# A delta-rule attention with a feed-forward behind it: the second inverse moved in front of the last weight conversion

## The chip, the cores and the metric

The kernel runs on one core of a Trainium2 chip. The metric is the device time of one execution, in microseconds (us). The kernel before takes 770.9 us (median of 3 runs, 770.83 to 771.04). The profile is of one more execution, which took 773.04 us; its span, from the first to the last instruction, is 771.3 us, and all positions in this document ("at 105 us") are counted from the start of a span.

The engines are called PE (TensorE, the matrix engine), DVE (VectorE), ACT (ScalarE), POOL (GpSimd) and SP (SyncE, which here only issues transfers).

## The reference, cut to what matters

For 4 batches and 8 heads, 768 positions of 48 values each, a state is updated by the delta rule:

```python
k_n = k / (np.linalg.norm(k, axis=-1, keepdims=True) + 1e-06)
for t in range(S):
    kt, vt, bt = (k_n[:, :, t], v[:, :, t], beta[:, :, t, None])
    y[:, :, t] = np.einsum('bhd,bhde->bhe', q[:, :, t], state)
    v_old = np.einsum('bhde,bhd->bhe', state, kt)
    state = state + bt[:, :, :, None] * np.einsum('bhd,bhe->bhde', kt, vt - v_old)
```

Its output, as 3072 rows of 384, goes through a feed-forward: `h = x @ w_in` (384 x 2048), `g = h * sigmoid(1.702 h)`, `out = g @ w_out` (2048 x 384). Everything is float32 in the kernel. `w_in` and `w_out` arrive as 64-bit floats, as two 32-bit words for each value, and the kernel builds the float32 values from the words itself.

## The kernel before, in words

**Units.** The 768 positions are cut into 6 chunks of 128. A chunk of one batch is a unit; units 0 to 3 are chunk 0, units 4 to 7 chunk 1, and so on. Inside a unit the delta rule is a triangular system. It is solved in four blocks of 32 positions: `solve` multiplies a block with the inverse of its 32x32 diagonal block (tile `XB`), ACT copies the result to `US`, `below` multiplies it with the Gram matrix `G` of the keys into `psR`, and `rest` (DVE) takes that off the values `V` of the blocks that follow. One such step of two interleaved units is called a hop (`hops`, `together`); eight hops solve a pair.

**Inverses.** `invert(c)` computes the 32x32 inverses of a chunk's units on DVE, with some 44 instructions that each follow from the one before. `invert(0)` is needed before the first hop; `invert(1)`, the second inverse, serves units 4 to 7. It reads the tile `NT`, which is filled by way of DRAM: for each unit, four transfers `Nd<-G` write the diagonal blocks of the Gram matrix, and one transfer `NT<-Nd` reads them back transposed. All of these are issued by SP.

**Keys.** `normalize_mixed` squares the keys on ACT (`ksq`), sums on DVE (`ssq`), takes the root on POOL (`rn`), and scales the keys on DVE. `prepare` then transposes them on PE (`psT`, copied to `kT`) and makes the Gram matrix (`psG`, copied to `G`), and issues the transfers to `NT`. The generator `keys` steps these for units 4 to 7 and for part of unit 8.

**Weights.** `conversions` turns the raw words into float32 on DVE, with one ACT operation per piece: 9 pieces of `w_in` (quarters 0, 1 and 3 of the 2048 columns are two pieces of 128x768 each, quarter 2 is three of 128x512) and then 14 pieces of `w_out` (twelve of 128x384, two of 128x768). `fill(n)` does n steps of that sequence; a piece has five steps. `fetch_in(3)`, the transfers of the last quarter of `w_in`, are issued by SP as soon as the second piece has been read.

**Feed-forward.** `hidden` makes `gT` for two batches; one step of it (`feed()`) is three products into `ph`, which the profile shows as 6 matmuls of 128x256, and it needs the attention output `xT`, whose last rows arrive through six transfers `xT<-last` that SP issues. `both_written(0, ...)` multiplies with `w_out` for two batches at once, in the order in which the pieces of `w_out` are converted.

**Order of the work.** The order on each engine is that of the program text for all that is pinned (`keep_in_program_order`), which is everything up to unit 8 or so; SP's transfers are pinned there as well. The part that the change touches is this sequence in the kernel's text:

1. loads, `invert(0)`, the first hops (units 0 and 1, line 1026), with `fill`, `keys` and `warm(11)` in every hop (`warm` is matmuls on nothing of use; each `warm(11)` is 11 of them),
2. `put_out` of units 0 and 1 (queries and state, PE tiles `psY`),
3. the second hops (units 2 and 3, line 1056), with `fill`, two steps of `keys`, and a `feed()` in each hop from the fourth on, `put_out` of units 2 and 3,
4. the scores of unit 4 (`first.scored`: tiles `QS`, `psQ`, `M`, and a subtraction from `V` on DVE),
5. `invert(1)` with 19 feeds beside it (line 1093),
6. the remaining feeds with the conversion of `w_out`, and then `woven`, which runs the steps of all further units with `both_written` and everything after it.

Scratch tiles of the tag `gT` are a ring of eight (`spare`), which `blocks` (the diagonal blocks of the first chunk), the raw words of quarter 2 and the `gT` tiles share. There are seven key tiles `KN`, so unit 7's keys need the tile of unit 0.

## Time and profile before

| what | value |
|---|---|
| median of 3 runs | 770.9 us |
| the profiled execution, its time | 773.04 us |
| the profiled execution, its span | 771.3 us |
| PE busy over the span | 751.0 us (97%) |
| DVE busy over the span | 440.6 us (57%) |
| ACT, POOL busy over the span | 241.3 us, 128.4 us |
| first hop begins, on PE | 42.1 us |
| second inverse, on DVE | 105.5 to 132.6 us |
| last instruction of the `w_out` conversion ends, on DVE | 172.4 us |
| `ps_warm` matmuls | 161 |

The page of the profile gives busy time for each engine, for the span and for forty slices of it (19.3 us each). The view by stretches gives busy time for stretches that the reader chooses. The view of waits says which engine stood still for whom. The chain of waits is followed back from the last instruction: at each step to what released it. A matmul that the program writes once in float32 is shown as two.

### The profile page before, as it was taken

Reading aid. Unit: us, or ns where it says so; the run is one execution under the profiler, and the core shown is the slowest. Engines: PE = TensorE matmul, PEld = TensorE weight load, DVE = VectorE, ACT = ScalarE, POOL = GpSimd, SP = SyncE. Lnnn points to the kernel's source line nnn. Section 1 sums busy time; section 2 is a strip of 40 time slices with the busy share of each in tenths; the row PEclk is TensorE's granted clock in tenths of the full one; section 3 lists DMA queues with packets and bytes.
Section 4 is the critical chain, followed back from the end, with each engine's and each line's share of the span. In section 5 each row is a group of like instructions: output and inputs, shape, how many; then the busy total and the mean of one; then the engine's idle time right before and its main releaser. Section 6 shows DMA issues by size and latency. Waiting matters only on the chain.

```text
span 771.3 us, 19547 instructions
## 1 busy us (share of the span) xinstructions
PE 751.0 (97%) x8545; PEld 563.6 (73%) x8545; DVE 440.6 (57%) x896; ACT 241.3 (31%) x535; POOL 128.4 (17%) x134
## 2 busy tenths in 40 slices
PE   7889999889999999999999999999999999999998
PEld 6678788556687688678678678678678677687684
DVE  5997879896875565665665665665665621000000
ACT  4555632343333233233223223233223123121110
POOL 6133310011221221220221221231210000000000
PEclk8588999999999999999999999999999999999999
DMA  9976550644342142142142042042030020000000
GB/s 158 176 119 144 123 97 21 165 101 97 77 108 57 35 95 57 35 97 56 27 103 56 23 107 58 23 98 66 22 77 12 23 45 1 17 11 1 26 1 20
DMA packets 130661, 50.78 MB, mean 66 GB/s; under 512 B 105408, under 2 KB 126016, under 8 KB 130576
## 3 DMA queue, kind: packets, MB, share of 16 engines
q1 hardware_dynamic: 128112, 41.08, 24.9%
q0 software_dynamic: 2464, 8.46, 4.6%
q8 instruction: 67, 1.10, 0.6%
q14 instruction: 18, 0.15, 0.1%
HBM read 32.08 MB, written 16.25 MB: 63 GB/s over the span
## 4 chain that ended last, share of the span: by engine, by line
PE 81%; DVE 10%; SPq 4%; ACT 2%; DMA 1%; issue 1%; POOL 0%; DVEq 0%; ACTq 0%
PE po L102 30%; PE ph L102 27%; PE psY L102 6%; PE psU L102 5%; SPq L102 4%; PE psQ L102 3%; PE psG L102 3%; PE psR L102 3%; DVE w_out L102 2%; DVE P L102 2%; PE psT L102 2%; PE ps_warm L102 2%; DVE tmp L102 2%; DVE YB L102 1%; DVE NT L102 1%
## 5 line engine op out<-in xcount | busy, mean ns | idle before, releaser
L102 PE MATMUL po<-w_out,gT 128*128 128x384 f32 x768 | 265.2, 493 | 3.6 <-ACT gT L102 1.9
L102 PE MATMUL ph<-xT,w_in 128*128 128x256 f32 x1152 | 260.9, 383 | 0.3
L102 PEld LDWEIGHTS ph<-xT,w_in 128*128 128x128 f32 x1152 | 214.9, 190 | 32.6 <-issue 1.7
L102 PEld LDWEIGHTS po<-w_out,gT 128*128 128x128 f32 x768 | 141.3, 190 | 94.2 <-issue 3.1
L102 DVE TENSOR_TENSOR V<-V,psR 128x384 f32<-128x384 f32 (+2 forms) x72 | 40.1, 558 | 193.6 <-PE psR L102 193.1
L102 ACT ACTIVATE gT<-ph 128x512 f32<-128x512 f32 x96 | 56.4, 595 | 138.9 <-PE ph L102 138.8
L102 DVE TENSOR_TENSOR P<-NT,YB 64x8 f32<-64x8 f32 (+26 forms) x178 | 86.0, 483 | 4.9
L102 ACT COPY US<-psU 32x384 f32<-32x384 f32 x92 | 43.1, 469 | 138.8 <-PE psR L102 81.6
L102 PEld LDWEIGHTS psU<-V,XB 32*32 32x32 f32 x1536 | 60.1, 106 | 34.6 <-issue 27.6
L102 DVE TENSOR_REDUCE YB<-P 64x4 f32<-64x8 f32 (+27 forms) x178 | 77.2, 434 | 6.1
L102 PE MATMUL psU<-V,XB 32*32 32x48 f32 x1536 | 71.5, 205 | 0.6 <-DVE V L102 0.4
L102 PE MATMUL psR<-US,G 32*32 32x48 f32 x2576 | 64.2, 205 | 1.5 <-ACT US L102 1.5
L624 POOL TENSOR_SCALAR_AFFINE_SELECT M<-M 128x1024 f32<-128x1024 f32 x20 | 25.5, 1276 | 225.6 <-DVE M L102 166.8
L102 PEld LDWEIGHTS psR<-US,G 32*32 32x32 f32 x2576 | 54.6, 105 | 2.8 <-ACT US L102 1.6
L102 PE MATMUL psQ<-QS,kT 48*128 48x176 f32 (+1 forms) x384 | 37.6, 341 | 3.7 <-ACT QS L102 3.7
L102 DVE TENSOR_TENSOR P<-NT 64x256 f32<-64x256 f32 (+7 forms) x44 | 36.3, 826 | 0.5
L102 DVE TENSOR_REDUCE NT<-P 64x64 f32<-64x1024 f32 (+7 forms) x44 | 35.3, 803 | 1.5
L102 PEld LDWEIGHTS psQ<-QS,kT 48*128 48x128 f32 x384 | 31.1, 209 | 6.8 <-ACT QS L102 5.5
L102 PE MATMUL psG<-kT 48*128 48x128 f32 x384 | 32.8, 309 | 2.7 <-ACT kT L102 1.4
L102 PEld LDWEIGHTS psG<-kT 48*128 48x128 f32 x384 | 27.6, 208 | 5.9 <-ACT G L102 2.2
L102 ACT COPY o<-po 128x384 f32<-128x384 f32 x24 | 11.5, 477 | 61.7 <-issue 39.2
L102 ACT COPY M<-psQ 128x256 f32<-128x256 f32 x68 | 22.8, 377 | 23.4 <-DVE V L102 17.3
(100 smaller groups left out, 605.4 us busy)
## 6 DMA issues: line engine op xcount, KB each, us to landing
Nd<-G SPq DMA_DIRECT2D x16, 512.0 KB, 3.5
QP<-in_q_dram SPq DMA_DIRECT2D x24, 192.0 KB, 3.8
V<-in_v_dram SPq DMA_DIRECT2D x24, 192.0 KB, 3.2
out_dram<-o SPq DMA_DIRECT2D x24, 192.0 KB, 2.4
KN<-in_k_dram POOLq DMA_DIRECT2D x15, 192.0 KB, 3.7
NT<-Nd SPq DMA_DIRECT2D x20, 128.0 KB, 2.8
Yd<-YS SPq DMA_DIRECT2D x20, 128.0 KB, 2.5
XB<-Yd SPq DMA_DIRECT2D x20, 128.0 KB, 3.3
```

What stands on the lines that cost most here:

```text
L102: return lambda *a, **kw: tc.keep_in_program_order(op(*a, **kw))
L624: (pool if self.n < B else nc.gpsimd).affine_select(out=self.M, in_=self.M, compare_op=ALU.is_gt, fill=0.0, base=0, pattern=[[0, H], [1, 1 ...
```

## The change

It moves work around in steps 1 to 6 above and adds no arithmetic.

- **Loads.** The keys of units 4, 5 and 6 are loaded in front of the second quarter of `w_in`, and the values of units 2 and 3 behind that quarter. The keys of unit 7 go into the tile `blocks`, after its first use, so they need not wait for `KN` of unit 0; `normalize_mixed` gets a second argument, and reads the raw keys there and writes the scaled ones to `KN`.
- **Keys.** `keys` is stepped twice in every hop of both pairs and once in each of the first two `put_out`s; the units begin at steps 0, 4, 8, 12 and (unit 8) 24 of a list of 34.
- **Fewer fills.** A hop now does one and two steps of the conversion in turn, instead of two, or three. When the second inverse begins, 36 steps have been taken (7 of the 9 pieces of `w_in`), where all of `w_in` and most of the first piece of `w_out` had been converted.
- **Fewer warm matmuls.** From the fourth of the first hops on, `warm` has 5 matmuls; the second hops have two times 5 instead of three times 11. In all there are 108 instead of 161.
- **Feeds.** The two halves' `hidden` are interleaved: three quarters of the first, three quarters of the second, then the rest of both. A feed stands in each of the second hops from the third on. During the second inverse there are 16 feeds and, between them, the scores of unit 4; the remaining 8 feeds, which need the last quarter of `w_in`, come behind the inverse, and so does the conversion of that quarter.
- **Transfers.** The loads of unit 4's queries and values are issued in the third of the second hops instead of the sixth.

```diff
-    for b in range(B):
+    for b in range(HB):
         load_values(b, sync)
-    fetch_in(1, other_queue)
-    D_ = spare("blocks").rearrange("p (b h k) -> p b h k", b=B, k=BS)
-    fetch_in(2, other_queue)
     for n in range(B, len(KN)):
         load(n, ((KN, k),), sync)
+    fetch_in(1, other_queue)
+    for b in range(HB, B):
+        load_values(b, sync)
+    blocks = spare("blocks")
+    D_ = blocks.rearrange("p (b h k) -> p b h k", b=B, k=BS)
+    fetch_in(2, other_queue)
...
+    seventh = blocks[:, 0 : H * D].rearrange("p (h d) -> p h d", h=H)
+    load(len(KN), (([seventh], k),), sync)
...
-        for t in range(24):
-            for u, begin in enumerate((0, 4, 7, 10, 13)):
+        for t in range(34):
+            for u, begin in enumerate((0, 4, 8, 12, 24)):
...
     for i in range(2 * NB):
         together(*next(path))
-        fill(2 if i else 5)
-        if 2 <= i < 6:
-            values_scaled(pair[HB + (i - 2) // 2], range((i - 2) % 2 * NP, (i - 2) % 2 * NP + NP))
+        fill(1 + i % 2 if i else 5)
+        ahead_of(preparing, 1)
+        if 4 <= i < 8:
+            values_scaled(pair[HB + (i - 4) // 2], range(i % 2 * NP, i % 2 * NP + NP))
         if i in (3, 5):
             pair[HB + (i - 3) // 2].select()
-        if i > 0:
-            ahead_of(preparing, 1)
-        warm(NU)
+        warm(NU if i < 3 else NU // 2)
+        ahead_of(preparing, 1)
     for n, s in enumerate(pair[:2]):
         put_out(s, 2 - n)
-        load(len(KN) + n, ((KN, k),), other_queue)
+        ahead_of(preparing, 1)
         fill(1 + n)
+    load(len(KN) + 1, ((KN, k),), other_queue)
...
-    ffn.append(hidden(xTs[0], gTs[0], slice(0, NTH), 1.3, True))
+    def some(work, n):
+        for _ in range(n):
+            yield next(work)
+
+    hiddens = [hidden(xTs[h], gTs[h], slice(0, NTH), 1.3, True) for h in range(HB)]
+    for w in hiddens:
+        ffn.append(some(w, 3 * FQ))
+    ffn += hiddens
     path = hops(*pair[2:])
     for i in range(2 * NB):
         together(*next(path))
-        fill(2 if i < 5 else 3)
+        fill(1 + i % 2)
         ahead_of(preparing, 1)
-        if i > 2:
+        if i > 1:
             feed()
         else:
-            warm(NU)
+            warm(NU // 2)
...
-        if i == 5:
+        if i == 2:
             load(B, ((QP, q),), sync)
             load_values(B, sync)
     for s in pair[2:]:
-        put_out(s, 2)
+        put_out(s, 1)
         feed()
-        fill(1)
-    ffn.append(hidden(xTs[1], gTs[1], slice(0, NTH), 1.3, True))
...
     first = new_step(B)
-    next(first.scored)
-    t = 0
-    while not ("in", 3, 1) in done:
-        fill(2)
-        feed()
-        if t == 1:
-            run(first.scored)
-        ahead_of(preparing, 1)
-        t += 1
     run(preparing)
-    run(first.scored)
     inverting = invert(1)
-    for i in range(19):
+    for i in range(22):
         ahead_of(inverting, 1)
-        feed()
+        if i in (1, 3, 5):
+            next(first.scored, None)
+        if i < 16:
+            feed()
     run(inverting)
     while ffn:
         feed()
-        fill(3)
+        fill(2)
```

The `while not ("in", 3, 1) in done` loop that is taken out had no turn to do before: the fills of the hops had already converted that piece.

More of the change, by code (lines that the diff above doesn't have):

```diff
@@ L313, in normalize, with normalize_mixed @@
         yield 0.0
-    def normalize_mixed(n):
+    def normalize_mixed(n, raw=None):
         K = KN[n % len(KN)][:, :, 0:D]
+        raw = K if raw is None else raw
         ksq = wk.tile([128, H, D], F32, tag="ksq", name="ksq", bufs=1)
-        act.activation(ksq, K, ACT.Square)
+        act.activation(ksq, raw, ACT.Square)
         yield
@@ L326, in normalize_mixed @@
         vec.reciprocal(rn, rn)
-        vec.tensor_tensor(K, K, rn.broadcast_to([128, H, D]), op=ALU.mult)
+        vec.tensor_tensor(K, raw, rn.broadcast_to([128, H, D]), op=ALU.mult)
         yield
@@ L1004, in unit @@
         def unit(n):
-            yield from normalize_mixed(n)
+            yield from normalize_mixed(n, seventh if n == len(KN) else None)
             yield from prepare(n)
```

## The prediction

> **What bounds the kernel now.** I read the view by stretches first, then the waits, the chain, and last the time lines of SP and PE. In the stretches the columns after the length are busy time of PE, its weight loads, DVE, ACT and POOL.
>
> ```profile
> 42.90:69.90 27.00, 25.11 (x494) 20.01 (x492) 24.04 (x36) 14.45 (x36) 7.88 (x8) 0.81 0.51 88
> 69.90:96.30 26.40, 25.03 (x499) 20.55 (x495) 21.68 (x43) 16.35 (x31) 9.24 (x10) 1.00 0.66 161
> 96.30:105.50 9.20, 8.26 (x99) 7.02 (x99) 5.88 (x14) 4.64 (x14) 0.55 (x1) 1.00 0.43 99
> 105.50:132.60 27.10, 27.10 (x127) 23.86 (x126) 25.76 (x44) 6.62 (x13) 1.42 (x1) 1.00 0.25 37
> 132.60:172.40 39.80, 34.77 (x360) 22.61 (x358) 36.78 (x80) 15.57 (x30) 4.51 (x3) 0.98 0.55 138
> 172.40:771.30 598.90, 594.66 (x6506) 440.65 (x6504) 291.95 (x613) 162.60 (x359) 88.16 (x68) 1.00 0.21 49
> ```
>
> The rows are the first hops with their outputs, the second hops, outputs and scores, the second inverse, the conversion of w_out, and the rest. In the rest PE is busy 594.66 of 598.90 us, and the waits of PE from 172.4 us on hold one line of 0.2 us. So the kernel is PE-bound from 172.4 us, the change moves none of that work, and **what it can move is the moment at which the last piece of w_out is converted**. From 42.9 to 172.4 us DVE is the fullest engine but for PE in the inverse: idle 2.96 + 4.72 + 3.32 = 11.0 us before the inverse, 1.3 in it, 3.0 after it, 15.3 in all. The chain goes through DVE there and changes to PE at the end of the conversion:
>
> ```profile
> 131.38 1.23 DVE YS L102
> 132.60 0.48 DVE w_out L102
> ...
> 146.41 0.18 DVE rn L102
> ...
> 169.46 0.61 ACT w_out L102
> 170.08 0.49 ACT kT L102
> 170.61 1.88 PE psG L102 x16
> 172.49 2.40 PE po L102 x4
> ```
>
> What DVE waits for in these 130 us (us in total, times, longest):
>
> ```profile
> DVE V L102 <- PE psR L102: 5.1, 6, 2.1
> DVE V L102 <- PE psQ L102: 2.7, 2, 2.5
> DVE ST L102 <- ACT xT L102: 1.8, 2, 1.3
> DVE rn L102 <- POOL rn L102: 1.8, 1, 1.8
> ```
>
> DVE's total work to that point is the same in both kernels, so the end moves by the change in DVE's idle time alone. That is the whole sum below.
>
> **What the Trainium skill says.** "DMA: Bandwidth & Descriptors", Two DMAs through the same engine are not ordered: the issuing engine has to wait for the first transfer's semaphore before it issues one that reads its data. So NT<-Nd holds up everything behind it on SP; the trace agrees (Nd<-G ends at 79.28 us, NT<-Nd goes at 80.64). "TensorE: Matmul & The Clock Gate", Part 1 (The HAM clock gate): PE's clock falls to half after an idle window of about 3.4 us, and rises after a busy one. The trace agrees in kind, and shows that a PE full of 32x32 products and of 11 warm matmuls per hop is not enough: the same 11 take 2.52 us at 57.7 us and 1.36 us at 65.8. The same page's first table: DVE and ACT take instructions strictly in order; so a DVE instruction that waits for PE stops the inverse behind it.
>
> **The sum, step by step.**
>
> 1. *Up to 42.9 us: 0.* DVE is in the first inverse until then, and no transfer that feeds it moves. The values of units 2 and 3 come later by some 5 us, but are read at the fifth hop, after 52 us. Unit 7's keys are one more load on SP ahead of the last quarter of w_in, and SP has nothing to do from 48.0 to 52.7 us; POOL loses one load. The second and third quarter's words land later by one and by three loads of 192 KB, and are read after 53 and 65 us, while DMA falls off from 45 us.
>
> 2. *First hops and outputs, +1.9.* DVE's 24.04 us stay (four wide pieces and the fifth's first operation, six rests) and gain the keys of units 4 to 7 where 1.4 units' were: 2.6 x (0.55 + 0.17 + 0.20 + 0.56) = 3.9, and one ST of 0.36: 28.3 us in a stretch of 27.0. So DVE now fills this stretch. I add 1.5 us for two waits on POOL's root (1.68 us each, half hidden): 42.9 + 28.3 + 1.5 = 72.7, against 70.8 for the same point before. The 53 fewer warm matmuls (some 0.12 us each at full clock) are no gain here: PE waits for DVE.
>
> 3. *Second hops and outputs.* DVE has only 13 us of work here, so PE sets the time. It starts at about 70, when its outputs are through (before: 69.98): 8 hops at 0.75 (the middle of 0.6 to 0.9 in the time line) = 6.0, two psT at 0.5 and one psG at 1.1, 10 warm 1.2, 8 feeds at 1.29 (6 matmuls of 0.216 start to start) = 10.3, two outputs at 1.5 = 3.0: 22.6. **A new wait comes in front of the first feed.** It needs xT, by way of SP, whose order is changed: before, xT<-last went ahead of the Nd and NT transfers, now two and a half units of them stand ahead of it.
>
> ```profile
> 52.69 6.23 SPq L102 DMA_DIRECT2D w_out<-in_moe_w_in_dram  x12
> 70.43 4.73 SPq L102 DMA_DIRECT2D xT<-last  x6
> 75.25 4.03 SPq L102 DMA_DIRECT2D Nd<-G  x4
> 80.64 0.31 SPq L102 DMA_DIRECT2D NT<-Nd  x1
> 81.48 8.28 SPq L102 DMA_DIRECT2D Nd<-G  x8
> 91.65 2.09 SPq L102 DMA_DIRECT2D Nd<-G  x4
> ```
>
> The 12 transfers of w_in go when the second piece is read, 1.7 us later than before (one key's 1.48 and a wait stand ahead), and end at 60.6. Then Nd of unit 4 (2.1 to 4.0 for four, I take 2.8) 63.4, a landing 1.4 and NT 0.3: 65.1; unit 5 the same: 69.6; Nd of unit 6: 72.4; six xT (3.7 and 4.7, I take 4.2): 76.6; the last lands 3.4 after its issue: 79.4. PE reaches its first feed at 70 + 2 hops 1.5 + psT, psG, warm 2.8 + third hop 0.9 = 75.3. It stands 4 us. The hop behind it waits too, since PE is in order. The second hops end at 96.6 with their last feed. ST of unit 3, ahead of the inverse on DVE, ends 2.36 us after its psY begins (before: 99.30 to 101.66), at 93.8 + 2.4 = 96.2. **The inverse begins at 96.3 instead of 105.5.** Its NT is there: unit 7's is issued by 83.
>
> 4. *The inverse, +5.0.* 27.1 as before, plus four subtractions of psQ from V (0.25 each, 0.8 together) that were ahead of it. They now stand among its first instructions, and PE has feeds queued ahead of psQ. From the start of psY (0): PE has outputs 1.5, feeds 1.3 + 1.3, psT 0.4, feeds 1.3 + 1.3, half of psQ 0.7: 7.8. DVE is at its first V at 2.4 + 3.3 = 5.7. It stands 2.2, and, with two more feeds ahead of the second half (PE 11.2, DVE 9.4), another 1.9; with the handover 4.2. It ends at 96.3 + 27.1 + 0.8 + 4.2 = 128.4, before: 132.6.
>
> 5. *Behind the inverse, +10.3.* Two wide pieces of w_in less their first operation: 8.3 by their rows (0.95, 0.96, 0.69, 0.95, 0.96), and 2.2 for w_out's first piece and the second's first operation; 0.2 is overlap. At the point where w_out's second piece would begin: 128.4 + 10.3 = 138.7 against 132.6, **6.1 us late**.
>
> 6. *Gained back, -1.8.* The wait for POOL's root at 144.6 goes: ten conversion instructions now stand between ssq and rn. 4.3 left.
>
> 7. *PE on the way, +1.7.* PE finishes 16 feeds and the scores at about 120 and has nothing until the eighth piece at 132, so it comes out at half clock; the 8 feeds (10.3 us, the first at double) end at 145, where before PE began po at 137.8. It has 29.6 us of work to there in the old trace and DVE needs until 176.7, so PE just keeps up; for rests that now find PE late I take 0.7, for a slow clock after the 4 us stand 1.0. Hidden only by DVE being slower: were PE's clock not to recover, each slow window of 3.4 us costs half of itself.
>
> Sum: **+6.0 us**, the profiled execution's span 771.3 to 777.3, its time 773.0 to 779.0; on the median of 770.9, **776.9 us**.
>
> **Bounds of what the trace does not show.** The stand for xT: 0 if SP gets xT out before the Nd transfers pile up, 7 if all four-groups take 4.0; I take 4. The psQ stand: 0 if DVE itself arrives late, 4.2 taken, 5 at half clock. A later landing of the third w_out piece, whose fetch now waits for the last quarter of w_in: 0 to 2, taken 0, since 5.5 us of conversion lie between (landing 4.0).
>
> **Rivals.**
>
> *Slow clock in the first hops.* With 5 warm matmuls and 48-row Gram products PE may fall to half clock from 54.8 to 70 us (before, it did so from 54.8 to 65, even with 11). A hop is then psU and psR 1.3, psG 2.2 or psT 1.0, warm 1.2: about 4.4 instead of 2.7 for four hops; SP's slack takes 1.5. Some 5 us more, 782. For it: the slow clock of before in the same hops. Against: more of PE's time is full-height products now, and fewer warm matmuls shorten a slow hop, which took 3.9.
>
> *The hops run at DVE's pace (faster).* DVE's work before the inverse is 51.6 - 11.5 = 40.1 us. If the wait on xT and PE's queue do not hold the second hops, the inverse begins as early as 83. It decides at 90.3: earlier than that the kernel is faster, by as much as the inverse is earlier. At 86 it is 767. For it: the scores (9.2 us in front of the inverse, 3.3 of them idle on DVE) are out of the way. Against: 22.6 us of PE work stand in the second hops.
>
> *It comes to nothing.* DVE's work is conserved, and the idle time only changes place: inverse at 90, 770.9.
>
> **How the numbers follow.** Within 0.2% (1.5 us) of the kernel before no measurement of it can tell a difference. The forecast, 773 to 779: 0.50. The slow clock, 779 to 786: 0.28. Nothing, 0.08; faster, 0.14. Slower 0.78, same 0.08, faster 0.14. The range leaves out the lower half of the faster case and the slow clock's end: 767 to 783.
>
> **What would show it.** Right: the inverse begins near 96; PE waits for xT some 4 us in front of the first ph; DVE waits on psQ some 4 us within the inverse; PE is idle some 12 us in front of the eighth piece's feeds; conversion ends near 177 to 178, and the rest takes 599 us. Wrong: the inverse begins before 91, or xT lands before PE asks; then the forecast falls on its third step. A rest other than 599 us would mean that PE's work did not stay the same.

## The result and the profile after

The changed kernel takes 792.0 us (median of 4 runs, 791.01 to 795.45) where the kernel before took 771.0 us beside it: a ratio of 1.0276 (95% interval 1.0242 to 1.031), or 21 us more. The forecast was 776.9 us, with a range of 767 to 783: the sign was right, and the size was a third of what came. The profiled execution took 795.45 us, its span is 793.7 us. Executions of one kernel below lie up to 9 us from its median (`after_warm`), and the stretches in which PE runs at half clock differ between profiles of the same instructions (below); so times are compared as ratios with intervals, and single waits by stretches of the profile.

The view by stretches of the changed kernel, in the columns of the prediction (length, busy time of PE, its weight loads, DVE, ACT and POOL, granted clock of PE, DMA share, GB/s). The rows are the first hops with their outputs, the second hops with theirs, the second inverse, the two late pieces of `w_in`, the conversion of `w_out`, and the rest:

```profile
42.20:73.60 31.40, 26.72 (x558) 22.27 (x556) 27.73 (x46) 19.95 (x49) 9.40 (x8) 0.89 0.46 101
73.60:109.30 35.70, 29.25 (x479) 23.00 (x478) 14.54 (x29) 11.96 (x25) 6.01 (x9) 0.81 0.41 112
109.30:140.90 31.60, 23.88 (x120) 19.96 (x118) 25.02 (x47) 7.52 (x15) 1.25 (x1) 0.94 0.23 35
140.90:151.00 10.10, 5.54 (x13) 4.50 (x14) 9.55 (x14) 0.94 (x1) 0.55 (x1) 0.50 0.63 136
151.00:193.50 42.50, 38.55 (x372) 25.72 (x371) 37.19 (x80) 17.18 (x33) 4.75 (x3) 0.94 0.40 107
193.50:793.70 600.20, 594.65 (x6506) 440.59 (x6504) 292.38 (x613) 162.79 (x359) 88.83 (x68) 1.00 0.21 49
```

The last row is the old one with 1.3 us more. So the loss lies in front of 193.5 us, as the prediction said it would. DVE has the same work to there as before, but stands idle for 3.7 + 21.2 + 6.6 + 0.5 + 5.3 = 37.3 us of it, where it was 15.3 us: the end of the conversion moves by the change in DVE's idle time, 22.0 us less 0.7 for the earlier begin of the first row, and it did move by 21.1 (172.4 to 193.5). The second row is the surprise: DVE is busy for 14.5 of 35.7 us there, PE for 29.2, the clock is 0.81 and DMA at 0.41, so nothing is full.

The chain of waits of the changed kernel (start, length, what), from the end of the inverse to the end of the conversion:

```profile
139.78 1.23 DVE YS L102
...
142.86 1.47 DVE w_in L102 x2
145.46 13.33 PE ph L102 x48
...
191.74 1.95 PE psG L102 x16
193.69 2.32 PE po L102 x4
```

Eight feeds in one block now lie on the chain, behind the last pieces of `w_in`. The waits of DVE from 42.9 to 200 us (us in total, times, longest), and then of PE:

```profile
DVE V L102 <- PE psR L102: 16.6, 6, 8.8
DVE ST L102 <- ACT xT L102: 6.3, 4, 3.3
DVE V L102 <- PE psQ L102: 5.6, 2, 3.4
DVE ssq L102 <- ACT ksq L102: 2.4, 1, 2.4
DVE w_out L102 <- ACT w_out L102: 2.1, 3, 1.5
```

```profile
PE ph L102 <- DVE w_in L102: 12.3, 1, 12.3
PE ph L102 <- DMA Nd<-G: 5.7, 1, 5.7
```

The wait on `psR` was 5.1 us and is 16.6: DVE stands for the hops, and the hops stand for a feed. That feed is the first; in the time line of PE it reads (start, length, operation, times, and in brackets the idle time in front of it):

```profile
84.20 2.90 PE L102 MATMUL ph<-xT,w_in 128*128 128x256 f32 x6 [5.70 <-DMA Nd<-G]
```

The name in the bracket is that of the last event of its queue. What the feed needs is `xT`, which lands then (in other runs below the bracket names `xT<-last`). The queue of SP, and the sizes and landing times of transfers from 72 to 90 us (KB each, median us from issue to landing):

```profile
72.15 2.50 SPq L102 DMA_DIRECT2D Nd<-G  x4
74.70 4.05 SPq L102 DMA_DIRECT2D xT<-last  x6
78.85 0.52 SPq L102 DMA_DIRECT2D NT<-Nd  x1
79.41 4.58 SPq L102 DMA_DIRECT2D Nd<-G  x4
```

```profile
w_out<-in_moe_w_out_dram POOLq DMA_DIRECT2D x4, 384.0 KB, 4.8
raw<-in_moe_w_out_dram POOLq DMA_DIRECT2D x1, 384.0 KB, 8.5
...
KN<-in_k_dram POOLq DMA_DIRECT2D x1, 192.0 KB, 8.2
...
xT<-last SPq DMA_DIRECT2D x6, 16.0 KB, 7.2
```

The six small transfers take 7.2 us to land. They leave while 2 MB that POOL has asked for are on the way. That is not new: in the kernel before, the same six took 6.4 us, beside the same four fetches and two loads of keys, and the first feed did not wait for them (landing, POOL's time line and PE's, of the kernel before):

```profile
xT<-last SPq DMA_DIRECT2D x6, 16.0 KB, 6.4
```

```profile
68.27 2.25 POOL L102 DMA_DIRECT2D w_out<-in_moe_w_out_dram  x4
70.51 1.98 POOL L102 DMA_DIRECT2D KN<-in_k_dram  x2
```

```profile
81.19 1.46 PE L102 MATMUL ph<-xT,w_in 128*128 128x256 f32 x6
```

What is new is when PE asks. Counted from the first outputs, the six begin to leave at 1.1 us instead of 0.4 us ahead of them, and PE asks for its first feed at 4.9 us (78.5) instead of 10.4, since the feed stands one hop earlier and behind fewer warm matmuls. At the old distance, 84.0 us, it would have waited 0.2 us.

PE is at half clock from 82.7 to 96.4 us, from before the end of the stand: a feed takes 2.90 us and not 1.56.

### The profile page after: what moved, and what is told of

Its sections match the earlier page's. It is cut to its first block, busy times and chain, and to the rows that moved or that the text cites. A ratio compares the mean times of both kernels' runs of the same rounds, so it can differ in the third digit from the quotient of the medians.

```text
span 793.7 us, 19441 instructions
## 1 busy us (share of the span) xinstructions
PE 753.6 (95%) x8492; PEld 564.4 (71%) x8492; DVE 440.9 (56%) x896; ACT 241.4 (30%) x535; POOL 127.4 (16%) x133
## 3 DMA queue, kind: packets, MB, share of 16 engines
q0 software_dynamic: 2400, 8.26, 4.2%
## 4 chain that ended last, share of the span: by engine, by line
PE 78%; DVE 11%; SPq 5%; DMA 3%; issue 1%; ACT 1%; POOL 0%; DVEq 0%; ACTq 0%
PE po L102 29%; PE ph L102 29%; PE psY L102 6%; SPq L102 5%; PE psU L102 4%; PE psQ L102 3%; PE psG L102 2%; PE psR L102 2%; DVE w_out L102 2%; DVE tmp L102 2%; PE psT L102 2%; DVE P L102 2%; DMA Nd<-G 1%; DVE YB L102 1%; DVE NT L102 1%
## 5 line engine op out<-in xcount | busy, mean ns | idle before, releaser
L102 PE MATMUL ph<-xT,w_in 128*128 128x256 f32 x1152 | 268.7, 390 | 18.3 <-DVE w_in L102 12.3
L102 PEld LDWEIGHTS ph<-xT,w_in 128*128 128x128 f32 x1152 | 218.9, 194 | 52.7 <-ACT w_in L102 12.7
L102 DVE TENSOR_TENSOR V<-V,psR 128x384 f32<-128x384 f32 (+2 forms) x72 | 40.1, 557 | 205.3 <-PE psR L102 204.9
L102 PEld LDWEIGHTS psU<-V,XB 32*32 32x32 f32 x1536 | 60.4, 107 | 35.5 <-issue 29.2
L102 ACT COPY US<-psU 32x384 f32<-32x384 f32 x92 | 43.2, 470 | 134.6 <-PE psR L102 80.9
L102 PE MATMUL psG<-kT 48*128 48x128 f32 x384 | 34.4, 321 | 2.7 <-ACT kT L102 1.4
L102 PEld LDWEIGHTS psG<-kT 48*128 48x128 f32 x384 | 29.3, 219 | 5.9 <-ACT G L102 2.1
L102 ACT COPY o<-po 128x384 f32<-128x384 f32 x24 | 11.5, 479 | 61.7 <-issue 39.2
```

Source lines behind the costliest of these rows:

```text
L102: return lambda *a, **kw: tc.keep_in_program_order(op(*a, **kw))
```

## The experiments

All runs are listed here with four moments of their profiles: the first outputs through (end of the second `ST`), the begin and the end of the second inverse, and the end of the conversion of `w_out`. Ratios are to the kernel before on the same chip; its own median was 771.0 to 773.3 us on the chips used, so medians of different rows are not to be compared to the last microsecond.

| run | median us | ratio, 95% | outputs | inverse | its end | converted |
|---|---|---|---|---|---|---|
| before | 771.0 | | 70.8 | 105.5 | 132.6 | 172.4 |
| after | 792.0 | 1.0276, 1.0242 to 1.031 | 73.6 | 109.3 | 141.0 | 193.5 |
| xt_pool | 785.1 | 1.0159, 1.0095 to 1.0222 | 73.4 | 102.9 | 134.6 | 187.1 |
| xt_key | 783.6 | 1.0134, 1.0088 to 1.018 | 73.2 | 97.7 | 129.4 | 180.9 |
| warm_wait | 788.6 | 1.0197, 1.0141 to 1.0253 | 77.0 | 106.1 | 137.8 | 189.2 |
| fetch_late | 786.9 | 1.0197, 1.016 to 1.0233 | 73.2 | 99.7 | 131.4 | 183.3 |
| scores_late | 791.9 | 1.0207, 1.0138 to 1.0277 | 77.3 | 113.5 | 141.4 | 194.6 |
| warm_gap | 793.2 | 1.0243, 1.0185 to 1.0301 | 76.8 | 108.6 | 140.4 | 191.7 |
| after_root | 792.1 | 1.0253, 1.0223 to 1.0284 | 76.7 | 108.2 | 139.9 | 189.7 |
| after_fill | 788.4 | 1.0189, 1.016 to 1.0217 | 77.0 | 109.9 | 142.5 | 188.6 |
| xt_key_sc_fill | 779.5 | 1.008, 1.0057 to 1.0104 | 75.6 | 103.1 | 130.7 | 178.5 |
| b_order | 782.8 | 1.0127, 1.01 to 1.0154 | 68.3 | 102.0 | 127.9 | 179.2 |
| b_keys | 775.4 | 1.0041, 1.0023 to 1.0058 | 75.8 | 108.0 | 135.0 | 174.2 |
| b_keys_warm | 772.0 | 0.9995, 0.9971 to 1.0019 | 73.0 | 104.9 | 131.9 | 171.1 |
| after_warm | 787.4 | 1.0213, 1.0151 to 1.0275 | 72.6 | 102.7 | 134.4 | 186.2 |
| mended | 781.1 | 1.0105, 1.0075 to 1.0135 | 75.8 | 101.1 | 129.0 | 180.2 |
| mended_warm | 778.9 | 1.0087, 1.0056 to 1.0118 | 74.3 | 101.3 | 129.1 | 179.7 |
| b_root | 769.6 | 0.9958, 0.9944 to 0.9972 | 68.3 | 103.6 | 130.7 | 168.9 |
| b_keys_root | 775.1 | 1.0024, 1.0012 to 1.0037 | 72.6 | 104.0 | 131.0 | 172.4 |

My theory after the result was that three things had been undersized: the stand for `xT`, the half clock behind it, and the stretch behind the inverse. The rival for each stood in the expectations.

### The second hops

**xt_pool**: the last rows of `xT` are sent by POOL.

```diff
-                    dmas = [sync, sync]
+                    dmas = [other_queue, other_queue]
```

> The changed kernel with one edit: the twelve xT<-last transfers of the first chunk are issued by POOL instead of SP, so they stand behind no NT<-Nd and ahead of the four w_out fetches in POOL's own queue. The cause in question: PE stood 5.7 us for xT (until 84.2 us) and then ran 13.7 us at half clock, so the second inverse began at 109.3 instead of the forecast 96.3. If the stand comes from SP's order and the fetches that collide with it, xT lands near 80, PE does not stand over 3.4 us, no slow clock follows, the inverse begins at 97 to 100, and as DVE's idle time decides, the end moves by as much: 780 to 783 us against 792.0 of the changed kernel. Rival, PE-bound behind the inverse (8 feeds and po against 42 us of conversion): the inverse begins early but the conversion still ends near 190, 788 to 792. Rival, xT is late because the DMA engines are full from 75 to 84 us whatever queue it is on: PE still stands until 83 or later, 790 to 793.

PE's stand for `xT` is gone (first feed at 78.3 us), and so is the long half clock. But the inverse began at 102.9 us, 5 us later than in the next run, because another wait took its place. In the time line of ACT:

```profile
87.14 0.52 ACT L102 ACTIVATE ksq<-KN 128x384 f32<-128x384 f32 x1 [5.39 <-DMA KN<-in_k_dram]
```

ACT stands for the keys of unit 8, whose load POOL now issues behind six more transfers and which landed 8.3 us after its issue; the copy to `US` for the next hop is queued behind it, and PE waits 3.6 us for that. The time of 785.1 us lies between what the cause and what its first rival had led me to expect.

**xt_key**: the same, with the load of unit 8's keys ahead of the fetches of `w_out`.

```diff
         ahead_of(preparing, 1)
+        if n == 1:
+            load(len(KN) + 1, ((KN, k),), other_queue)
         fill(1 + n)
-    load(len(KN) + 1, ((KN, k),), other_queue)
```

> The changed kernel with xT<-last issued by POOL, and the load of unit 8's keys in POOL's queue moved ahead of the four w_out fetches. With xT alone moved, PE no longer stood for it, yet the second hops and their outputs still took 29.5 us (from the second ST to the inverse's first instruction; 35.7 in the changed kernel): ACT stood 5.4 us at ksq for unit 8's keys, whose load was issued behind xT and the w_out fetches and landed 8.3 us later, and the copy to US behind it in ACT's queue held up the hop. If that is the next wait, it goes, the stage takes 23 to 25 us (the forecast's 23.6), the inverse begins 4 to 6 us earlier and the time is 779 to 782. Rival, the stage is held by PE's own length and the clock: still 28 to 30 us, 784 to 786.

The second hops of that kernel, in the view by stretches:

```profile
73.20:97.72 24.52, 23.76 (x479) 19.01 (x478) 14.56 (x29) 11.98 (x25) 9.22 (x16) 1.00 0.79 196
```

They take 24.5 us instead of 35.7, at full clock, with PE busy for all but 0.8 us. So 11.2 us of the changed kernel's second hops are waiting and half clock, with the work unchanged. PE asks for its first feed at 78.1 us here, and needs 19.6 us from there to the inverse. The stage came out as expected, the time 1.6 us above the range.

**warm_wait**: 45 warm matmuls in front of the first feed, so that PE is not idle while it waits.

```diff
         if i > 1:
+            if i == 2:
+                warm(45)
             feed()
```

> The changed kernel with 45 matmuls on nothing of use in front of the first feed (about 5.4 us at full clock), in the 5.7 us in which PE stands for xT anyway. It parts the stand from the slow clock behind it. If the slow clock is what costs (three feeds at 2.86 us instead of 1.30, three and a half hops at 1.3 instead of 0.75: 6.6 us), the stand stays but the first feeds take 1.3 to 1.5 us, the inverse begins at 102 to 104, and the time is 785 to 787. If the slow clock is of no account because the hops wait for ACT and DVE, or the end is set elsewhere: 791 to 793.

The stretch falls from 35.7 to 29.1 us with the wait still in it, at full clock. From the start of the first feed to the inverse it is 19.3 us instead of 25.1, so 5.8 us were half clock after the stand; the other 0.8 us are `xT`, which came sooner behind the outputs. The time was 788.6 us, above what I expected; in the profile the first outputs come 3.4 us later (below). The Trainium skill's "TensorE: Matmul & The Clock Gate", Part 1 (The HAM clock gate), states a fall to half clock after an idle window of about 3.4 us. That agrees: after a stand of 5.7 us the clock fell, and with the stand filled it did not. How long it stayed down differs by execution: in the five profiles with a stand of 4.2 to 6.2 us at this place (`after`, `scores_late`, `warm_gap`, `after_root`, `after_warm`) half clock lasted 13.7, 17.1, 6.9, 6.8 and 3.4 us, and the way from the first feed to the inverse was 5.5, 5.5, 1.2, 1.2 and 1.6 us longer than the 19.6 of `xt_key`.

**fetch_late**: `xT` stays on SP in its changed place, and the four fetches of `w_out` go later. This separates the place in SP's queue from the traffic beside it.

```diff
-        ("in", 1, 1): lambda: (fetch_out(4), fetch_out(5), fetch_out(6), fetch_out(7)),
...
+        if i == 4:
+            for f in (4, 5, 6, 7):
+                fetch_out(f)
         if 3 <= i < 6:
             fetch_out(i - 3)
```

> xT<-last stays on SP in its changed place; the four fetches of w_out pieces 4 to 7 (384 KB each by POOL at 73 to 75 us) go only at the fifth of the second hops. If xT was late because its six transfers shared the DMA engines with these fetches (landing 7.2 us instead of 3.4 to 3.8), xT is in at 79 to 80.5, PE stands at most 1.5 us in front of its first feed, the slow clock after the stand goes, the inverse begins at 97 to 101 and the median is 780 to 785. If its place on SP behind two and a half units of Nd was the cause, it still lands at 83 to 84, PE stands 5 us and the median is 790 to 793.

Time lines of SP and of PE, and the landing time:

```profile
74.27 3.77 SPq L102 DMA_DIRECT2D xT<-last  x6
```

```profile
80.33 1.53 PE L102 MATMUL ph<-xT,w_in 128*128 128x256 f32 x6 [2.09 <-DMA xT<-last]
```

```profile
xT<-last SPq DMA_DIRECT2D x6, 16.0 KB, 3.5
```

The transfers leave at almost the same moment (74.27 against 74.70) and land in 3.5 us instead of 7.2. The first feed begins at 80.3 and not 84.2; the stand of 2.1 us is shorter than the window, the clock holds, and the inverse begins 9.6 us earlier. The conversion ends 10.2 us earlier in the profile; by the ratios the gain is some 6 us, and the median misses the 780 to 785 by 2. The collision with the fetches is shown as the cause of the long landing. It is not shown as what the change brought, since the kernel before had it too; there the later feed hid it. With the fetches out of the way a stand of 2.1 us stays: SP sends the six from 74.3 us, where POOL in `xt_key` sends them from 73.1.

### Within the inverse

**scores_late**: unit 4's scores at the end of the inverse.

```diff
-        if i in (1, 3, 5):
+        if i in (16, 18, 20):
```

> The changed kernel with the three parts of unit 4's scores at turns 16, 18 and 20 of the inverse's loop instead of 1, 3 and 5, so that they come behind all 16 feeds on PE, and the subtractions on DVE stand near the end of the inverse. If DVE's stand for psQ (3.4 + 2.2 us) counts in full, the inverse takes 27 to 28 us instead of 31.7 and the time is 786 to 788. If that idle time only changes place (the pieces of w_in and PE's feeds behind the inverse are the bound), 791 to 793.

DVE's two stands for `psQ` (5.6 us) became one of 2.3, and the inverse took 27.9 us instead of 31.7. The time stayed at 791.9 us, with runs from 785.9 to 795.2: the profile has half clock from 52.8 to 73.3 and from 83.5 to 100.6 us, more than the changed kernel itself. So the gain is shown in its stretch and not in the time, which is the rival's.

### Behind the inverse

**warm_gap**: 100 warm matmuls between the inverse and the late feeds.

```diff
     run(inverting)
+    warm(100)
     while ffn:
```

> The changed kernel with 100 matmuls on nothing of use behind the second inverse (about 12 us at full clock), in the 12.3 us in which PE stands for the eighth piece of w_in. If the slow clock there costs time by way of ACT (gelus that wait for slow feeds hold up the w_out steps queued behind them on ACT: DVE stood 2.4 + 2.1 us), the 8 feeds take 10.4 us instead of 13.3, DVE's 4.5 us go, and the time is 787 to 789. If DVE's conversions set the pace whatever PE does there: 791 to 793. The warm matmuls begin only when PE has done its 16 feeds, at about 132.7, so they should end before 145.5.

The eight feeds ran at full clock (144.8 to 156.8 us), but the stretch from the inverse to the end of the conversion only fell from 52.5 to 51.3 us, and the time of 793.2 us is the rival's. Half clock is not what makes it long.

**after_root**: the squares of unit 9's keys go ahead of the late gelus on ACT; their sums follow with the last feeds.

```diff
+    early = normalize_mixed(2 * B + 1)
+    next(early)
     run(inverting)
     while ffn:
         feed()
+        if len(ffn) == 1:
+            next(early, None)
         fill(2)
```

(`woven` then takes `early` for that unit and does its remaining step.)

> The changed kernel with the same: unit 9's squares ahead of the late feeds' gelus on ACT. If ACT's order costs time behind the inverse, DVE's wait on ksq (2.4 us) goes, the stretch from the end of the inverse to the end of the conversion falls from 52.5 to 50 us and the median to 789 to 790.5. If PE's late feeds set the pace there, the wait only changes its name: 52 us or more, 791 to 793.

The stretch fell to 49.8 us, as expected. DVE's wait for `ksq` is gone, and a wait of 1.3 us for the root came back. The median did not fall (792.1); the ratio is 0.2% lower with intervals that overlap. In the profile the first outputs are 3.1 us later than in the changed kernel's, with half clock from 52.9 to 73.4, which takes up the gain. By time this stays open.

**after_fill** and **xt_key_sc_fill**: more conversion steps in the second hops, so that more of `w_in` is ready in front of the inverse; the second has `xt_key` and `scores_late` as well.

```diff
-        fill(1 + i % 2)
+        fill(2)
...
-        put_out(s, 1)
+        put_out(s, 2)
         feed()
+        fill(1)
```

> The changed kernel with nothing but the conversion put back in front of the second inverse: two conversion steps in every second hop and three in each output behind them. PE still stands for xT and runs at half clock. As DVE is idle for 12.7 us of that stage, the 8.3 us of w_in's last quarter cost nothing there and are gone behind the inverse, and PE does not stand for the eighth piece: conversion ends 8 to 11 us earlier, 781 to 784. Rival, the stage grows by what is put in: 789 to 793.

> The previous kernel with, besides, the scores of unit 4 at turns 16, 18 and 20 of the inverse's loop, and two conversion steps in every second hop and three in each output behind them, so that all but two operations of w_in are converted in front of the second inverse. If DVE has some 10 us of idle time in second hops that PE sets the length of, the conversions are free there: the inverse begins at 97 to 99, takes 28, and then only w_out's 14 pieces remain (40 us): conversion ends at 165 to 168, and the time is 763 to 767, below the kernel before. Rival, the conversion steps hold up the rests of the hops on DVE and ACT: the inverse begins at 105 or later, 771 to 776.

In `after_fill` the second hops did not grow (32.9 us, with 6.6 us more work of DVE in them), so the additional steps cost nothing beside the stand for `xT`. (In the combined kernel, which has no such stand, the second hops take 27.4 us, 2.9 more than in `xt_key`.) Behind the inverse DVE is busy 6.5 us less (40.1 and not 46.7 us), and the stretch fell by as much, from 52.5 to 46.1 us. The ratio fell by 0.0087, some 7 us; the median of 788.4 us lies above the 781 to 784 of the expectation and below its rival. The combined kernel was to come in under the kernel before and came in 0.8% above it, above both of its cases. Its PE time line behind the inverse (which ends at 130.7 us):

```profile
133.67 10.76 PE L102 MATMUL ph<-xT,w_in 128*128 128x256 f32 x36 [3.73 <-DVE w_in L102]
144.27 4.34 PE L102 MATMUL po<-w_out,gT 128*128 128x384 f32 x12
```

The products with `w_out` (`po`) begin 13.6 us after the inverse; before, it was 5.2 us (137.8 against 132.6). PE is busy for 25.9 of the 27.6 us of the inverse, then stands 3.7 us for the last piece of `w_in`, and still has 6 feeds to do, in part at half clock (132.4 to 139.2 us). So even with nearly all of `w_in` converted in front, feeds that wait for its last piece hold up what follows on PE.

### The two halves of the change

**b_order**: the kernel before with the order alone: seven of nine pieces of `w_in` in front of the inverse, the feeds interleaved, the last quarter and eight of the feeds behind. Keys, loads and warm matmuls are those of before.

```diff
-        fill(2 if i < 5 else 3)
+        fill(1 if i else 2)
...
-    while not ("in", 3, 1) in done:
...
     for i in range(19):
         ahead_of(inverting, 1)
-        feed()
+        if i < 17:
+            feed()
```

> The kernel before with one part of the change alone: the second inverse in front of w_in's last quarter (36 conversion steps ahead of it), both halves' first three quarters of the feed-forward ahead of or beside it (7 + 17 feeds) and the last quarter behind. Keys, loads, warm matmuls, the scores in front of the inverse and the order of SP's first transfers are those of before. If this order is free because DVE's work is conserved, the inverse begins 8 to 10 us earlier, ends as much earlier, and the conversion ends within 2 us of before: 769 to 773. If the order itself costs, by the 8 feeds and the clock that come behind the inverse (DVE waits there were 4.5 us in the changed kernel): 774 to 778. If most of the 21 us were in this part: 785 or more.

From the outputs to the inverse, first in the kernel before and then in this one, and this one's inverse and what follows it:

```profile
70.80:105.50 34.70, 32.39 (x577) 26.75 (x578) 26.65 (x54) 20.45 (x43) 8.89 (x9) 1.00 0.60 140
```

```profile
68.30:102.00 33.70, 31.63 (x571) 26.22 (x569) 17.15 (x41) 18.72 (x40) 9.64 (x10) 1.00 0.58 144
102.00:127.92 25.92, 21.84 (x102) 18.91 (x100) 24.89 (x44) 5.98 (x12) 1.42 (x1) 1.00 0.21 40
127.92:179.23 51.31, 41.62 (x386) 28.21 (x387) 46.60 (x94) 18.60 (x36) 5.31 (x4) 0.93 0.45 115
```

This half costs 1.27%, some 9.8 us, and its median lies between two of the cases that I had named. The rows, from the fastest of its four executions, say how: from the outputs to the inverse 33.7 us where it was 34.7, the inverse 25.9 where it was 27.1, and behind it 51.3 where it was 39.8. DVE has 9.5 us less to do in the first stretch, but PE is busy for 31.6 of its 33.7 us, so taking conversion off DVE there gives back 1.0 us of the 11.5 that are lost behind the inverse.

**b_keys**: the other half alone: loads in the new order, keys early, fewer warm matmuls. Its edit is the change's own diff down to the load of unit 8's keys, without what follows. Its core:

```diff
-        for t in range(24):
-            for u, begin in enumerate((0, 4, 7, 10, 13)):
+        for t in range(34):
+            for u, begin in enumerate((0, 4, 8, 12, 24)):
...
-        warm(NU)
+        warm(NU if i < 3 else NU // 2)
```

> The kernel before with the key half of the change alone: loads in the new order, keys of units 4 to 7 in the first hops, five warm matmuls from the fourth hop; scores, conversion and feeds keep the order of before (all of w_in converted in front of the inverse). If the two halves add, this costs what the whole change costs beyond the order half: 21 less 5 to 12, so 780 to 786, with the stand for xT in front of the first feed (3 to 6 us) and slow clock after it. If the key half does harm only together with the other (feeds one hop earlier, fewer conversions), the first feed finds xT landed, and the median is 770 to 774.

It costs 0.41%, some 3.2 us (775.4 us, just above the second case of the expectation), and `xT` is not late in it, though SP sends it no earlier:

```profile
76.92 3.95 SPq L102 DMA_DIRECT2D xT<-last  x6
```

```profile
86.35 1.56 PE L102 MATMUL ph<-xT,w_in 128*128 128x256 f32 x6
```

The order of before has its first feed one hop later and 11 warm matmuls in each of the hops ahead of it; PE asks 5.5 us after the last of the six is issued. That is 10.6 us behind the first outputs, as in the kernel before (10.4), and it does not wait: sent this late, `xT` makes no stand by itself.

The two runs cost 9.8 + 3.2 = 13.0 us of 21.3. The other 8.3 us have no run of their own, since the two halves leave out parts of the change: the first feed one hop earlier, 10 warm matmuls instead of 33 in the second hops, the scores within the inverse, and the earlier loads of unit 4. Of all profiles only those with the early feed have PE standing for `xT`, so the stand, its half clock and DVE's stands for `psQ` are the likely rest; a kernel with the early feed alone was not run.

### The clock in the first hops

**b_keys_warm** and **after_warm** lay 11 warm matmuls in every first hop again, instead of 5 from the fourth on.

```diff
-        warm(NU if i < 3 else NU // 2)
+        warm(NU)
```

> The key half alone, with all 11 warm matmuls in each of the first hops as before (the change lays 5 in the last five). If fewer warm matmuls let PE fall to half clock in the first hops (b_keys: from 54.0 to 71.1 us), the half clock is at most 10 us long, the second ST of the first pair ends at 71 to 73 instead of 75.8, and the median ratio to before falls from 1.0041 to 1.000 to 1.002. If warm matmuls don't set the clock there, half clock stays 14 us or more, or comes and goes by run alone, and the ratio stays 1.003 to 1.006.

> The changed kernel with all 11 warm matmuls in each of the first hops. If their number sets the clock there, the first hops end no later than 73.6 in any run and the ratio is 1.022 to 1.025 (profiles of the variants had the first outputs through at 76.4 to 77.3 where the clock was slow, 73.4 where it wasn't). If not, 1.0276 as it is, or more, since 53 more matmuls cost up to 0.12 us each where PE is the bound.

With them, the key half costs nothing (0.9995, where the interval without them began at 1.0023), and the whole change loses 0.63% less (1.0213), with intervals that overlap. (The second has 138 warm matmuls, 30 more than the changed kernel and not 53.) The clock's record in all profiles, as us at half clock between 50 and 76 us of the span:

| warm matmuls in a late first hop | us at half clock, by profile |
|---|---|
| 11 | before 10.3; b_order, b_root, b_keys_warm, b_keys_root, after_warm 0; mended_warm 3.4 |
| 5 | after 6.8; xt_pool 3.5; xt_key, fetch_late 3.4; b_keys, xt_key_sc_fill, mended 17.1; warm_wait, warm_gap, scores_late, after_fill, after_root 20.5 |

In the row of 5, where it is 17 to 20 us the outputs are through at 75.6 to 77.3 us; where it is 3 to 7, at 73.2 to 73.6. All values are multiples of the window of 3.4 us. "TensorE: Matmul & The Clock Gate", Part 1, of the Trainium skill calls the window free-running. That fits the second row: up to the first outputs its kernels run the same program text, and yet have 3.4 to 20.5 us. So the number of warm matmuls shifts the odds and does not settle one execution. Against expectation, `after_warm` still had a run of 796.3 us; the profile, of another execution, had the stand for `xT` (4.2 us).

### Whether the mends add

**mended** is the changed kernel with the edits of `fetch_late`, `scores_late` and `after_root`; **mended_warm** has that of `after_warm` too.

```diff
-        if i in (1, 3, 5):
+        if i in (16, 18, 20):
...
-        warm(NU if i < 3 else NU // 2)
+        warm(NU)
```

> Three waits of the changed kernel removed at once: the w_out fetches behind the xT transfers, scores at the inverse's sixteenth, eighteenth and twentieth step, unit 9's squares ahead of the late gelus. If they add up (10 us by fetch_late's profile, 2.3 by scores_late's, 2.7 by after_root's, the last two measured on stretches), the conversion ends at 178 to 180 and the median is 777 to 779.5, just where the forecast was, with PE's late feeds and the two late pieces of w_in as all that stays. If one wait takes another's place, the median is 782 to 786.

> The changed kernel with the three waits removed as in mended, and 11 warm matmuls in each of the first hops. If the two mends add, the first outputs are through at 73 instead of 75.8, the conversion ends at 176 to 178, and the ratio is 1.005 to 1.008 (776 to 778), where the forecast was; what stays is the stretch behind the inverse, some 49 us against 39.8. If they don't, 1.009 to 1.0105.

They add for the most part: 781.1 and 778.9 us, 1.0105 and 1.0087, 1.6 and 0.9 us above what I expected. In `mended` the second hops take 25.3 us, the inverse 27.9, and the stretch behind it 51.2; in `mended_warm` that stretch is 50.5, where I had expected some 49. The view by stretches of `mended`, from the last subtraction of scores behind the inverse to the end of the conversion:

```profile
131.20:180.20 49.00, 42.48 (x386) 29.04 (x387) 45.16 (x92) 18.39 (x35) 5.31 (x4) 0.92 0.44 115
```

DVE is busy for 45.2 of 49.0 us in it. What is left when the waits are gone is the work behind the inverse, 10.7 us more than before in `mended_warm`, of which the earlier inverse gives back about a third.

### A kernel faster than both

**b_root**: the kernel before, with unit 9's squares issued ahead of the end of the inverse and their sums two conversion steps behind it.

```diff
+    early = normalize_mixed(2 * B + 1)
+    next(early)
     run(inverting)
+    fill(2)
+    next(early)
     while ffn:
         feed()
         fill(3)
```

> The kernel before with the squares of unit 9's keys issued before the end of the inverse and their sums two conversion operations behind it, so that the root on POOL lies beside conversions. If the wait for it (1.8 us at 144.6) is on the path that sets the end, the conversion of w_out ends 1.8 us earlier and the median is 768.5 to 769.8, a kernel faster than both. If another wait takes its place, 770.5 to 772.5.

```profile
131.44 0.55 DVE L102 TENSOR_REDUCE ssq<-ksq 128x8 f32<-128x384 f32 x1
...
143.94 0.17 DVE L102 TENSOR_SCALAR rn<-rn 128x8 f32<-128x8 f32 x1
```

12 us lie between the sums and the first use of the root, and DVE's wait of 1.8 us is gone. From the end of the inverse to the end of the conversion it is 38.2 us, 1.6 less than before. The ratio is 0.9958 (0.9944 to 0.9972), 3.2 us: faster than both kernels, and more than the wait explains. The rest is not settled; this profile has no half clock at 171 us, where that of before has one window, and none in the first hops either, which the edit does not touch.

**b_keys_root**: `b_keys_warm` with the same edit.

```diff
+    early = normalize_mixed(2 * B + 1)
+    next(early)
     run(inverting)
+    fill(2)
+    next(early)
```

> The kernel before with the key half, all 11 warm matmuls, and the root laid beside conversions as in b_root. If the key half is neutral, the ratio is that of b_root, 0.995 to 0.998 (769 to 770.5). If the earlier keys have used up what b_root gains, 0.999 to 1.001.

It is slower than before (1.0024), which neither side of the expectation held. In PE's time line:

```profile
140.87 5.19 PE L102 MATMUL po<-w_out,gT 128*128 128x384 f32 x10 [4.06 <-ACT gT L102]
```

PE stands 4.1 us for a gelu and then has half clock from 141.0 to 144.4 us; in `b_root` that stand is 1.7 us and the clock holds. The conversion ends at 172.4, not 171.1. That the stand costs more here because it is longer than a window fits both profiles, but was not tested.

## Why the prediction failed

The frame held. The rest of the kernel took 600.2 us (forecast 599), DVE's work was conserved, and the end moved by DVE's idle time. One reading under it was wrong: DVE is not the fullest engine up to the inverse. In the prediction's own first three lines PE is fuller, with 25.11, 25.03 and 8.26 us against 24.04, 21.68 and 5.88; so DVE's time in front of the inverse was worth less than it looked (`b_order`). By the prediction's own steps, in us of the profile:

| step | forecast | measured | miss |
|---|---|---|---|
| 2, first outputs through | +1.9 | +2.8 | 0.9 |
| 3, from there to the inverse | -11.1 | +1.0 | 12.1 |
| 4, the inverse | +5.0 | +4.6 | -0.4 |
| 5 to 7, behind the inverse | +10.2 | +12.7 | 2.5 |
| the rest | 0 | +1.3 | 1.3 |
| sum | +6.0 | +22.4 | 16.4 |

(-11.1 is 23.6 less the 34.7 us of before; +10.2 is 10.3 less 1.8 plus 1.7. The changed kernel's profiled execution was 3.4 us above its median, so the forecast of the median misses by 15.)

**Step 3 is the one that failed.** It named the right wait in the right place, and mis-sized three terms: the landing of `xT`, the half clock behind the stand (which it left to step 7) and PE's own work.

- *The landing of `xT`.* Step 3 forecast it 6.7 us after the first outputs; it was 10.6. Of the difference of 3.9, 1.3 us are that the last of the six left later than the sum had it (4.6 us behind the outputs, not 3.3), and 2.6 us are the landing itself. The 3.4 us for that is the median over two groups of six in the trace before: the six in question, at 70 us beside the fetches, took 5.0 to 7.0 us, the six at 101 us took 1.7 to 1.8, and none took 3.4 (lines below). So the long landing stood in the trace that the sum was made from; `fetch_late` shows what it comes from, 7.2 us that became 3.5 when the 384-KB fetches left later. The stand came out at 5.7 us, forecast 4, for PE too asked later than summed (4.9 us behind the outputs, not 2.6).
- *The half clock after the stand.* Step 7 expected the clock to fall and put it at 1.0 us; in the changed kernel's profile it is 5.5 (35.7 less the 24.5 of `xt_key` less the stand of 5.7), or 5.8 by `warm_wait`. Half clock lasted 13.7 us, four windows, in which PE ran the hops and feeds at half speed. In three other profiles with such a stand it cost 1.2 to 1.6 us, near the forecast, and the changed kernel's profile is of its slowest execution; so the size of this term varies, and the table has a large one.
- *PE's own work.* From the first feed to the inverse PE needs 19.6 us at full clock (`xt_key`); the sum had 16.9. The feeds begin 2.3 us apart there, where the sum has 0.75 + 1.29 = 2.04 for a hop and a feed.

Together 3.9 + 5.5 + 2.7 = 12.1 us. The landing of `xT<-last` in the kernel before, for 40 to 180 us and then for 60 to 90 us alone:

```profile
DMA to landing us min/median/max: 1.7/3.4/7.0
```

```profile
DMA to landing us min/median/max: 5.0/6.4/7.0
```

**Step 4 was right** in kind: DVE stands for `psQ` twice, 5.6 us together against 4.2. That the inverse took 31.7 us, forecast 32.1, is in part luck: DVE's work in it came out some 1.4 us shorter than summed (25.2 us busy with the subtractions, where before it was 25.7 without their 0.8). **Step 5 was right** for the conversions: the point it names came 11.8 us behind the inverse, of which 10.3 are conversion and 1.5 are a wait that it left out. A gelu of the late feeds stands ahead of the conversion's operation on ACT. **Step 6 was wrong**: the wait for POOL's root did go, and one of 2.4 us for `ksq`, behind the same gelus on ACT, took its place (`after_root` takes it out: 2.7 us on the stretch). **Step 7's** forecast of PE's idle time in front of the late feeds, some 12 us, was met: 12.3.

**Step 2 and the slow-clock rival.** The rival of half clock in the first hops, with 5 us and a chance of 0.28, did happen, beside the forecast and not instead of it. In the changed kernel's own profile it is only 6.8 us long, and step 2 is off by 0.9; with 11 warm matmuls back the ratio falls by 0.0063, about 5 us, an interval of about that size. The case against it in the prediction, that full-height products would keep the clock up, fell with the table. The two other rivals are out: no inverse began before 97 us in any version with this order.

What the prediction got wrong as a whole was to treat its cases as alternatives. The stand, its half clock, the first hops' half clock and ACT's order all point the same way and came together; the range ended where the first of them did.

## What to carry to other kernels

When work is moved to where it asks for a transfer sooner, read how long that very transfer took in the old trace and what flew beside it; a median over all transfers of the same name can mix two situations (6.4 and 1.8 us here). When a forecast contains a stand of PE of about a clock window or more, charge half clock behind it, as a range: here 1.2 to 5.5 us behind stands of 4.2 to 6.2. And work taken off an engine only helps in a stretch which that engine bounds: in `b_order` 9.5 us of DVE's work, moved out of hops that PE paced, gave back 1 us there, and the stretch that they went to grew by 11.5.

## What the runs showed of the hardware

- Six transfers of 16 KB between on-chip tiles take 7.2 us to land (median) with four fetches of 384 KB under way, and 3.5 with these sent later (`fetch_late`). In the kernel before, two such groups of six take 6.4 us beside the same fetches and 1.8 without them. A load of 192 KB goes from 4.6 to 8.2.
- PE full of small products does not always hold its clock: with 5 warm matmuls a hop it was at half clock for 3.4 to 20.5 us in the first hops, with 11 for 10.3 at most and mostly not at all.
- Behind a stand of 4.2 to 6.2 us at the first feed, half clock lasted 3.4 to 17.1 us (five profiles). After one of 2.1 us it did not begin (`fetch_late`), after one of 1.3 us it lasted 3.4 us (`mended_warm`).
